# Left-over tokens of a head pair in both partition halves, and the last output tile stored by column halves

## The chip, the cores and the metric

The kernel runs on one core of one Trainium2 chip. A core has a matmul engine (TensorE, PE in the profile, with its weight loads listed apart as PEld), a vector engine (VectorE, DVE), a scalar engine (ScalarE, ACT), GpSimd (POOL) and SyncE (SP), which here only issues transfers. Operands lie in on-chip memory of 128 partitions (SBUF); matmuls write to a second on-chip memory of 128 partitions (PSUM), which is divided into banks of 512 fp32 values a partition. The metric is the device time of one execution in microseconds (us), the median of several.

## What is computed

Attention with a softmax on q along the head dimension and one on k along the tokens, and behind it a two-layer network on all tokens:

```python
batch, n_heads, seq, head_dim = (8, 8, 576, 64)
q_s = softmax(q, axis=-1); k_s = softmax(k, axis=2)          # each with + 1e-09 in the denominator
kv = np.einsum('bhsd,bhse->bhde', k_s, v)
attn = np.einsum('bhsd,bhde->bhse', q_s, kv)
x = attn.transpose(0, 2, 1, 3).reshape(4608, 512)
r = np.maximum(x @ w_in, 0.0)                                # w_in 512 x 2048
out = (s * (r * r) + b) @ w_out                              # w_out 2048 x 512
```

All of it is fp32. A head has 576 tokens: four tiles of 128 and a left-over of 64 (`LEFT`).

## The kernel before

**The network.** The 4608 tokens are worked on as eight blocks of 512 tokens (`TB`), one for each batch, and a ninth block that collects the 64 left-over tokens of all eight batches. A block takes 16 steps, one for each 128 columns of w_in. A step is twelve 128x512 matmuls for `h` (L998: four chunks of the contraction, three products each, since every fp32 operand is split in a high and a low part) and twelve for the output, `acc` (L1061). Between them ACT takes the relu of h (L1023), DVE squares and scales (L1036), ACT rounds to the high part gh (L1038) and DVE takes the rest gl (L1040). In the last full block and the ninth, h is made by products of half-size blocks (L875), and the ninth block's output by `final` (L984).

**Attention** is done beside that, one block ahead. Heads come in "pairs" of transfers, `pr` = 0 to 15, of four heads each (two units `u`, two heads in each). `load_heads` and `load_v` (L284 to L298) bring k, q and v of a pair from memory into one tile each: token tiles 0 to 3 in all 128 partitions, and the left-over tile `NQ` (= 4) of all four heads in partitions 0 to 63. Partitions 64 to 127 of that tile are held at zero by memsets (L294, L499, L578), so that a matmul over all 128 partitions adds nothing there. For pairs 2 to 15, `k_pair` and `k_late` take the maximum of k over the tokens in DVE steps (L472, then L475 and L476, or L508 and L509 where the second works on the left-over tile alone), subtract it (L491, L538) and take the exponential (L498, L576).

**The kv product** of a pair is `heads` (L306): for each of the two units i, for each of the five token tiles n, for each of the two heads h, one matmul with the tile's 128 partitions as contraction, 64 columns of k as weights and 65 columns of v (64 values and a column of ones, which gives the softmax's denominator) as the moving operand. That makes 20 fp32 matmuls, each of which the chip runs as two instructions, 40 in the trace. Head 0 writes to PSUM partitions 0 to 63 and head 1 to 64 to 127, so each uses one half of the array's columns. Both units' results lie in one bank, in the PSUM tile "sm". DVE (L654, L655, L661) scales the result into the block-diagonal kvf, ACT and POOL split it (L668, L670), and `x_late` multiplies it with the transposed q (xp and xq, L690) into a two-bank tile "big" and a one-bank tile "sm". Pairs 0 and 1 take another way (`k_stream`, `kv_stream`), in which k arrives transposed.

**The order** on each engine is not that of the code. Each piece of work is a generator that yields an `Op` with its engine, an estimated cost in us, a due step, the things it needs and the PSUM or SBUF tiles that it takes and frees. `Order.run` (L161) builds the program by always choosing the operation that can start earliest by these estimates, and among near ones the one with the earliest due step. So a changed cost or another tile moves other work as well. Each engine then runs its instructions strictly in that order, with semaphores for what it depends on.

**The end.** `leave_last(j)` (L1080) copies the finished PSUM tile j of the ninth block into SBUF, by ACT (by DVE for j = 2), and stores it as two transfers of 64 tokens each, 128 KB, one issued by SP and one by ACT.

Of the kernel before, what the change touches and what calls it, by code (L numbers as in the profile page):

```python
# [8 lines left out]
F32 = mybir.dt.float32  # L9
# [16 lines left out]
def attention_moe(ctx: ExitStack, tc: tile.TileContext, q, k, v, w_in, w_out, s, b, out):  # L26
# [257 lines left out]
    def load_heads(pr, which, eng, i=0, n=4):  # L284
# [2 lines left out]
        eng.dma_start(t[:, :, 0:NQ, :], main(src, i, n))  # L287
        eng.dma_start(t[0:LEFT, :, NQ, :], left(src, i, n))

    def load_v(pr):  # L290
        main, left = sources(pr)
        vt, rest = v_tile(tiles[pr][2])
        if pr == NP // 2:
            nc.gpsimd.memset(rest[LEFT:P, :, 0:D], 0.0)  # L294
            nc.gpsimd.memset(tiles[pr][2][:, 0:VW].rearrange("p (m e) -> p m e", e=D + 1)[:, :, D:D + 1], 1.0)
        for h in range(4):
            nc.sync.dma_start(vt[:, h, :, 0:D], main(v, h, 1)[:, 0])
        nc.sync.dma_start(rest[0:LEFT, :, 0:D], left(v, 0, 4))  # L298

    def copier(eng):  # L300
        return nc.scalar.copy if eng == "ACT" else nc.vector.tensor_copy
# [4 lines left out]
    def heads(kv, kt, vt):  # L306

        for i in range(2):
            for n in range(NT):
                for h in range(2):  # L310
                    nc.tensor.matmul(  # L311
                        kv[h * D:(h + 1) * D, i], kt[:, i, h, n], vt(2 * i + h, n), start=(n == 0), stop=(n == NT - 1)
                    )

    def scales(z, src):

# [45 lines left out]
    def k_pair(pr):  # L362
        us = (2 * pr, 2 * pr + 1)
        due = DUE_K[us[0]]

        def sm(n):
            return ps.tile([P, 512], F32, name=f"{n}_{pr}", tag="sm", bufs=1)

        yield Op("DVE", 0.69, due, needs=[f"k{u} there" for u in us])
        kt = by_head(tiles[pr][0])  # L370
        kts = [kt[:, 2 * i:2 * i + 2] for i in range(2)]
        m2, m1, km = k_tiles(pr)
        k_max_2(kt, m2)
# [12 lines left out]
        for i, u in enumerate(us):  # L386
            yield Op("ACT", 0.63, due, gives=[f"k{u}"])
            k_exp(kts[i])

    def kv_second(pr):  # L390
        due = DUE_V[pr]
        yield Op("PE", 1.4, due, needs=[f"k{u}" for u in (2 * pr, 2 * pr + 1)] + [f"v{pr} there"], take=["sm"], gives=[f"kv{pr}"])
        kv = ps.tile([P, 512], F32, name=f"kv_{pr}", tag="sm", bufs=1)[:, 0:2 * (D + 1)].rearrange("p (u e) -> p u e", u=2)
        heads(kv, by_head(tiles[pr][0]).rearrange("p (u h) n d -> p u h n d", u=2), v_at(tiles[pr][2]))
# [3 lines left out]
        yield Op("ACT", 1.03, due, free=["sm"], gives=[f"kvf{pr}"])  # L398
        blocks(pr, kv[:, :, 0:D], z)

    def kv_stream(pr):
# [71 lines left out]

    def k_max_1(kt, m2, m1):
        nc.vector.tensor_tensor(out=m1, in0=m2[:, :, 0], in1=m2[:, :, 1], op=ALU.max)  # L475
        nc.vector.tensor_tensor(out=m1[0:LEFT], in0=m1[0:LEFT], in1=kt[0:LEFT, :, NQ], op=ALU.max)  # L476

    def k_turn(m1, kT):
        for i in range(2):
# [14 lines left out]
            op=ALU.subtract,  # L494
        )

    def k_exp(kt):
        nc.scalar.activation(kt, kt, AF.Exp)  # L498
        nc.gpsimd.memset(kt[LEFT:P, :, NQ], 0.0)  # L499


    maxima = {}
# [1 line left out]
    def k_max_0(kt, m2, m1):  # L504

        m2, kt = [t.rearrange("p h n (r t) -> p h n t r", t=2) for t in (m2, kt)]
        m1 = m1.rearrange("p h (t r) -> p h t r", t=2)
        nc.vector.tensor_tensor(out=m1, in0=m2[:, :, 0], in1=m2[:, :, 1], op=ALU.max)  # L508
        nc.vector.tensor_tensor(out=m1[0:LEFT], in0=m1[0:LEFT], in1=kt[0:LEFT, :, NQ], op=ALU.max)  # L509

    def k_turn_0(m2, m1):
        m = m2.rearrange("p h n d -> p (h n d)")[:, 0:4 * D]
# [58 lines left out]
    def k_exps(u):  # L571
        pr, i = divmod(u, 2)
        due = begin(pr)
        yield Op("ACT", 0.72, due, needs=[f"k{u} less"])
        kt = by_head(tiles[pr][0])[:, 2 * i:2 * i + 2]
        nc.scalar.activation(kt, kt, AF.Exp)  # L576
        yield Op("POOL", 0.2, due, gives=[f"k{u}"])
        nc.gpsimd.memset(kt[LEFT:P, :, NQ], 0.0)  # L578

    def q_late(u):  # L580
        pr, i = divmod(u, 2)
# [62 lines left out]
    def kv_late(pr):  # L644
        us = (2 * pr, 2 * pr + 1)
        due = begin(pr)
        yield Op("PE", 1.52, due - NFC, needs=[f"k{u}" for u in us] + [f"v{pr} there"], take=["sm"], gives=[f"kv{pr}"], late=WAIT)

        kt, _, vt = tiles[pr]
        kv = ps.tile([P, 512], F32, name=f"kv_{pr}", tag="sm", bufs=1)[:, 0:2 * (D + 1)].rearrange("p (u e) -> p u e", u=2)  # L650
# [5 lines left out]

        kvf = kvfs[pr % 2]
        for h in range(2):
            yield Op("DVE", 0.5, due, needs=[f"x{u - 4}" for u in us], free=["sm"] if h else ())
# [420 lines left out]
    def leave_last(j):  # L1080

        t = B * NFC + NFC * (j + 1)

        yield Op("DVE" if j == 2 else "ACT", 0.6, t, needs=[f"final {j}"])
        if not lasts:
            lasts.append(work.tile([P, AREA], F32, name="last", tag="area"))
        o = lasts[0][:, j * DO:(j + 1) * DO]
        (nc.vector.tensor_copy if j == 2 else nc.scalar.copy)(o, acc[B, j])  # L1088
        for i, (e, eng) in enumerate((("SP", nc.sync), ("ACT", nc.scalar))):
            yield Op(e, 0.1, t)  # L1090
            bb = 2 * j + i
            eng.dma_start(out[bb * S + TB:(bb + 1) * S, :], o[half[i]])
# [35 lines left out]
    def whole(pr, which, n, due=0, needs=()):  # L1128
        gives = [f"k{2 * pr} there", f"k{2 * pr + 1} there"] if which == 0 else [f"{n}{pr} there"]
        yield Op("SP", 1.3, due, needs=needs, gives=gives, kb=576)  # L1130
        load_heads(pr, which, nc.sync)

    def others():

# [21 lines left out]
    def reload(pr):  # L1156
# [2 lines left out]
        due = DUE_K[2 * pr] - 2  # L1159

        def v_():
            yield Op("SP", 3.2, due, needs=[f"kv{p}"], gives=[f"v{pr} there"], kb=1100)
# [4 lines left out]
    def reload_late(pr):  # L1167
# [3 lines left out]
        late = [f"q{u} turned" if pr > NP else f"qe{u}" for u in (2 * pr - 2, 2 * pr - 1)]  # L1171

        def k_():
            yield Op("SP", 1.3, due, needs=gone, gives=[f"ks{pr} there"], kb=576)
            load_heads(pr, 0, nc.sync)

        def q_():
            yield Op("SP", 1.3, due, needs=gone + late, gives=[f"q{pr} there"], kb=576)
            load_heads(pr, 1, nc.sync)

        def v_():
            yield Op("SP", 3.2, due, needs=gone, gives=[f"v{pr} there"], kb=864)
            load_v(pr)

        return k_(), q_(), v_()
# [67 lines left out]
```

## Time and profile before

| | |
|---|---|
| median of 3 runs | 859.88 us (859.0 to 860.23) |
| the profiled execution, device time | 860.12 us |
| the profiled execution, span from the first to the last instruction | 858.2 us |
| DVE, ACT, POOL busy | 590.8, 435.7, 164.4 us |
| HBM read and written | 60.29 and 18.40 MB, 92 GB/s over the span |

The device time of the profiled execution is 1.9 us more than its span. Busy times are the sums of the instructions of an engine; matmuls overlap in the pipeline, so their durations (about 390 ns for one of 128x512) are longer than the distance from one to the next, and what counts for the time is that distance, read from the starts. The rows that the argument rests on stand in the prediction.

### The profile page before, as it was taken

The numbers are of one execution on the slowest core, as the hardware profiler recorded it, in microseconds if no ns is written. First come the engines' busy times: TensorE is split into PE (matmuls) and PEld (weight loads), VectorE is DVE, ScalarE is ACT, GpSimd is POOL, SyncE is SP. The second block draws the span as 40 slices with busy tenths as digits, with TensorE's granted clock in tenths as the row PEclk, the third lists the DMA queues.
The fourth block names the chain that finished last, engine by engine and source line by source line (L and its number), as shares of the span: only waits on it lengthen the run. The fifth ranks groups of instructions, "written<-read, shape, count | busy, mean of one in ns | idle before, by whom it ended". The sixth has DMA issues, their size and how long they took to land.

```text
span 858.2 us, 11838 instructions
## 1 busy us (share of the span) xinstructions
PE 846.7 (99%) x4406; PEld 699.5 (82%) x4406; DVE 590.8 (69%) x922; ACT 435.7 (51%) x733; POOL 164.4 (19%) x184
## 2 busy tenths in 40 slices
PE   8899999999999999999999999999999999999997
PEld 6688888888888888888888888888888888888886
DVE  6999976778685857777587867685766587656300
ACT  5898744446364535454544454454336665555300
POOL 1000011111121110211020202120023436665000
PEclk9999999999999999999999999999999999999999
DMA  9994134334333324333424314421530110000100
GB/s 262 303 379 145 34 87 138 83 94 104 115 85 86 84 89 132 90 83 89 132 77 97 90 68 93 123 61 50 132 90 1 53 50 0 1 1 1 49 25 25
DMA packets 106573, 79.47 MB, mean 93 GB/s; under 512 B 56212, under 2 KB 100244, under 8 KB 106388
## 3 DMA queue, kind: packets, MB, share of 16 engines
q1 hardware_dynamic: 105364, 77.60, 32.4%
q10 hardware_dynamic: 1152, 1.11, 0.4%
q8 instruction: 35, 0.57, 0.3%
q14 instruction: 22, 0.18, 0.1%
HBM read 60.29 MB, written 18.40 MB: 92 GB/s over the span
## 4 chain that ended last, share of the span: by engine, by line
PE 94%; DMA 3%; DVE 1%; ACT 1%; issue 0%; SPq 0%; ACTq 0%
PE acc L1061 41%; PE h L998 35%; PE q L875 8%; PE last L984 5%; PE kv L311 2%; PE qa L875 1%; DMA st<-in_moe_w_out_dram 1%; DMA raw<-in_q_dram 1%; PE xp L690 1%; PE xq L690 1%; DMA area<-in_q_dram 1%; PE xp L454 0%; DVE low L232 0%; PE qT L444 0%; DVE w L239 0%
## 5 line engine op out<-in xcount | busy, mean ns | idle before, releaser
L998 PE MATMUL h<-x,w 128*128 128x512 f32 x1344 | 329.5, 391 | 0.8 <-DVE x L463 0.8
L1061 PE MATMUL acc<-w,gh 128*128 128x512 f32 x1024 | 317.7, 391 | 0.0
L998 PEld LDWEIGHTS h<-x,w 128*128 128x128 f32 x1344 | 250.1, 188 | 53.2 <-DVE x L463 1.4
L1061 PEld LDWEIGHTS acc<-w,gh 128*128 128x128 f32 x1024 | 190.9, 188 | 39.4
L1061 PE MATMUL acc<-w,gl 128*128 128x512 f32 x512 | 199.6, 390 | 0.1
L1023 ACT ACTIVATE r<-h 128x512 f32<-128x512 f32 x112 | 66.8, 596 | 170.8 <-PE h L998 168.3
L1036 DVE SCALAR_TENSOR_TENSOR r<-r,sb 128x512 f32<-128x512 f32 x106 | 84.5, 798 | 92.2 <-ACT r L1023 91.7
L1061 PEld LDWEIGHTS acc<-w,gl 128*128 128x128 f32 x512 | 96.1, 188 | 20.6 <-DVE gl L1040 0.5
L1038 ACT ACTIVATE gh<-r,sb 128x512 fp32r<-128x512 f32 x106 | 76.7, 724 | 53.8 <-DVE r L1036 52.9
L1040 DVE SCALAR_TENSOR_TENSOR gl<-r,sb,gh 128x512 fp32r<-128x512 f32 x106 | 83.2, 785 | 29.5 <-ACT gh L1038 28.6
L589 POOL TENSOR_TENSOR area<-area,qm 128x640 f32<-128x640 f32 x24 | 33.5, 1399 | 134.8 <-DVE qm L587 119.4
L606 POOL TENSOR_TENSOR qe<-qe,qr 128x640 f32<-128x640 f32 x24 | 32.3, 1348 | 75.9 <-DVE qr L602 41.1
L984 PE MATMUL last<-w 128*128 128x512 f32 x192 | 43.7, 389 | 0.0
L984 PEld LDWEIGHTS last<-w 128*128 128x128 f32 x192 | 36.1, 188 | 7.5
L670 POOL TENSOR_TENSOR spare<-kvf,spare 128x256 fp32r<-128x256 f32 x12 | 9.8, 820 | 129.9 <-issue 119.4
L696 ACT COPY y<-xp 64x320 f32<-64x320 f32 x48 | 20.2, 420 | 26.9 <-PE xp L690 26.5
L576 ACT ACTIVATE area<-area 128x640 f32<-128x640 f32 x24 | 17.6, 737 | 18.7 <-DVE area L538 18.7
L578 POOL MEMSET area<- 64x128 f32 x24 | 4.8, 200 | 116.2 <-issue 92.4
L958 DVE SCALAR_TENSOR_TENSOR gl<-r,sb,gh 128x512 fp32r<-128x512 f32 x16 | 13.7, 855 | 17.1 <-ACT gh L953 17.1
L700 DVE TENSOR_TENSOR y<-xp,y 64x320 f32<-64x320 f32 x48 | 23.4, 488 | 2.7 <-ACT y L696 1.7
L1088 DVE COPY last<-last 128x512 f32<-128x512 f32 x1 | 0.7, 692 | 34.6 <-PE last L984 34.6
L311 PEld LDWEIGHTS kv<-area 128*64 128x64 f32 x600 | 18.7, 137 | 5.1 <-issue 3.3
(190 smaller groups left out, 1073.4 us busy)
## 6 DMA issues: line engine op xcount, KB each, us to landing
st<-in_moe_w_in_dram SPq DMA_DIRECT2D x16, 512.0 KB, 8.3
st<-in_moe_w_out_dram SPq DMA_DIRECT2D x16, 512.0 KB, 9.0
out_dram<-o SPq DMA_DIRECT2D x16, 512.0 KB, 2.6
turned<-area SPq DMA_DIRECT2D x24, 320.0 KB, 2.3
qT<-turned SPq DMA_DIRECT2D x48, 160.0 KB, 3.1
area<-in_q_dram SPq DMA_DIRECT2D x14, 512.0 KB, 5.4
area<-in_k_dram SPq DMA_DIRECT2D x14, 512.0 KB, 4.3
area<-in_v_dram SPq DMA_DIRECT2D x56, 128.0 KB, 5.0
```

The source lines that it names most:

```text
L311: nc.tensor.matmul(kv[h * D:(h + 1) * D, i], kt[:, i, h, n], vt(2 * i + h, n), start=(n == 0), stop=(n == NT - 1))
L589: nc.gpsimd.tensor_tensor(out=qt, in0=qt, in1=bc(qm, [P, 2, NT, D]), op=ALU.subtract)
L606: nc.gpsimd.tensor_tensor(out=qe_, in0=qe_, in1=qr, op=ALU.mult)
L700: nc.vector.tensor_tensor(out=y[half[h], at], in0=parts[h][a][half[h]], in1=y[half[h], at], op=ALU.add)
L875: nc.tensor.matmul(BANK[where], w(a)[:, c * P:(c + 1) * P], xs[b_][:, c], start=k in (0, 1, 3) and n == 0, stop=n == 5, skip_group_check=True)
L984: nc.tensor.matmul(t_, g[:, js], w_, start=(f == 0 and i == 0), stop=(f == NFC - 1 and i == 2))
L998: nc.tensor.matmul(hp_, w[:, j, c, :], x[:, c, :], start=(c == 0 and i == 0), stop=(c == NP - 1 and i == 2))
L1023: nc.scalar.activation(r, hp_, AF.Relu)
L1036: nc.vector.scalar_tensor_tensor(out=r, in0=r, scalar=s_col, in1=r, op0=ALU.mult, op1=ALU.mult)
L1038: nc.scalar.activation(gh, r, AF.Identity, bias=b_col)
L1040: nc.vector.scalar_tensor_tensor(out=gl, in0=r, scalar=b_col, in1=gh.bitcast(F32), op0=ALU.add, op1=ALU.subtract)
L1061: nc.tensor.matmul(acc[blk, j // 2][:, j % 2], g[:, js], w_, start=(f == 0 and i == 0), stop=(f == NFC - 1 and i == 2))
```

## The change

Two things are changed.

First, for pairs 2 to 15, the left-over tile of k and v no longer lies in partitions 0 to 63 for all four heads. Heads 0 and 1 (unit i = 0) stay there, heads 2 and 3 (unit i = 1) go to partitions 64 to 127 (`half[i]`). Each of the two left-over transfers (k's and v's) becomes two, of two heads each. The kv product, now `heads_by_rows`, first does the 16 matmuls over 128 partitions (unit 0, then unit 1) and then the four left-over ones, each over the 64 partitions that hold its tokens. A 64-partition contraction with 64 weight columns uses a quarter of the array (64x64), and the four use four different quarters. The units' results now lie in two different banks: the product takes the two-bank tile "big" in place of "sm". The maximum over the left-over tile (L476, L509) becomes two DVE instructions of 64x128 in place of one of 64x256. The memset of v's unused half at pair 2 (L294) goes; k's memsets (L499, L578) stay and zero the other half. The estimated costs follow: the kv product 1.4 to 1.27 and 1.52 to 1.39, the loads with 0.65 more for each added transfer.

Second, the last output tile (j = 3) is copied by column halves, 256 columns by ACT and 256 by DVE, and each half leaves as one transfer of 128 tokens with 1 KB each, ACT's half issued by ACT and DVE's by SP.

```diff
+    def load_k(pr):
+        main, left = sources(pr)
+        t = by_head(tiles[pr][0])
+        nc.sync.dma_start(t[:, :, 0:NQ, :], main(k, 0, 4))
+        for i in range(2):
+            nc.sync.dma_start(t[half[i], 2 * i:2 * i + 2, NQ, :], left(k, 2 * i, 2))
+
     def load_v(pr):
...
-            nc.gpsimd.memset(rest[LEFT:P, :, 0:D], 0.0)
...
-        nc.sync.dma_start(rest[0:LEFT, :, 0:D], left(v, 0, 4))
+        for i in range(2):
+            nc.sync.dma_start(rest[half[i], 2 * i:2 * i + 2, 0:D], left(v, 2 * i, 2))
...
+    def heads_by_rows(kv, kt, vt):
+
+        at = [(i, n, h, slice(0, P)) for i in range(2) for n in range(NQ) for h in range(2)]
+        at += [(i, NQ, h, half[i]) for i in range(2) for h in range(2)]
+        for i, n, h, rows in at:
+            nc.tensor.matmul(
+                kv[h * D:(h + 1) * D, i], kt[rows, i, h, n], vt(2 * i + h, n)[rows], start=(n == 0), stop=(n == NQ)
+            )
...
     def kv_late(pr):
...
-        yield Op("PE", 1.52, due - NFC, needs=[f"k{u}" for u in us] + [f"v{pr} there"], take=["sm"], gives=[f"kv{pr}"], late=WAIT)
+        yield Op("PE", 1.39, due - NFC, needs=[f"k{u}" for u in us] + [f"v{pr} there"], take=["big"], gives=[f"kv{pr}"], late=WAIT)
...
-        kv = ps.tile([P, 512], F32, name=f"kv_{pr}", tag="sm", bufs=1)[:, 0:2 * (D + 1)].rearrange("p (u e) -> p u e", u=2)
-        heads(kv, by_head(kt).rearrange("p (u h) n d -> p u h n d", u=2), v_at(vt))
+        kv = ps.tile([P, 2, 512], F32, name=f"kv_{pr}", tag="big")[:, :, 0:D + 1]
+        heads_by_rows(kv, by_head(kt).rearrange("p (u h) n d -> p u h n d", u=2), v_at(vt))
...
-        nc.vector.tensor_tensor(out=m1[0:LEFT], in0=m1[0:LEFT], in1=kt[0:LEFT, :, NQ], op=ALU.max)
+        k_max_left(kt, m1)
+
+    def k_max_left(kt, m1):
+        for i in range(2):
+            m, rest = m1[half[i], 2 * i:2 * i + 2], kt[half[i], 2 * i:2 * i + 2, NQ]
+            nc.vector.tensor_tensor(out=m, in0=m, in1=rest, op=ALU.max)
...
-        nc.gpsimd.memset(kt[LEFT:P, :, NQ], 0.0)
+        nc.gpsimd.memset(kt[half[1 - i], :, NQ], 0.0)
...
     def leave_last(j):
...
+        if j == NQ - 1:
+            rows = out.rearrange("(b s) e -> b s e", b=B)[2 * j:2 * j + 2, TB:S]
+            for e, eng, copy, es in (
+                ("ACT", nc.scalar, nc.scalar.copy, slice(0, DO // 2)), ("SP", nc.sync, nc.vector.tensor_copy, slice(DO // 2, DO))
+            ):
+                copy(o[:, es], acc[B, j][:, es])
+                yield Op(e, 0.1, t)
+                eng.dma_start(rows[:, :, es], o[:, es])
+            return
```

The same edits are made in `kv_second` (pairs 2 and 3) and in `k_exp`, `k_exps` and `k_max_0`; `whole` and `reload_late` call `load_k` for k.

The instructions in their order show three places. The first is PE at the kv product of pair 2 (names end in tile numbers; "waits" lists the semaphores by the engine or transfer queue that raises them). Before:

```order
L311 MATMUL kv_913<-area 64x65 [waits DMAHW0_49,DVE_49,DMAHW2_49,PE_49,Activation_49]
L311 MATMUL kv_913<-area 64x65 [waits DMAHW3_49]
L311 MATMUL kv_913<-area 64x65 x6
L311 MATMUL kv_913<-area 64x65 [waits DMAHW6_49,DMAHW1_49,Pool_49]
L311 MATMUL kv_913<-area 64x65
L311 MATMUL kv_913<-area 64x65 [waits DMAHW4_49,Activation_49]
L311 MATMUL kv_913<-area 64x65 [waits DMAHW5_49]
L311 MATMUL kv_913<-area 64x65 x6
L311 MATMUL kv_913<-area 64x65 [waits Pool_49]
L311 MATMUL kv_913<-area 64x65
```

And in the changed kernel:

```order
L327 MATMUL kv_915<-area 64x65 [waits DMAHW3_49,DMAHW0_49,Activation_49]
L327 MATMUL kv_915<-area 64x65 [waits DMAHW4_49]
L327 MATMUL kv_915<-area 64x65 x6
L327 MATMUL kv_915<-area 64x65 [waits DMAHW5_49,Activation_49]
L327 MATMUL kv_915<-area 64x65 [waits DMAHW6_49]
L327 MATMUL kv_915<-area 64x65 x6
L327 MATMUL kv_915<-area 64x65 [waits DMAHW7_49,DMAHW1_49]
L327 MATMUL kv_915<-area 64x65
L327 MATMUL kv_915<-area 64x65 [waits DMAHW2_49,DMAHW0_49]
L327 MATMUL kv_915<-area 64x65
```

The number of matmuls is the same, 20; the left-over ones, which stood at the end of each unit, now stand together at the end, wait for their own transfers and no longer for POOL's memset.

The second is PE some 1.5 steps behind the kv product of pair 4, where the first product with that pair's q (xp, xq) stands. Before, behind the last of a step's four groups of acc:

```order
L1061 MATMUL acc_2_1457<-w_559,gh_1558 128x512 x2
L1061 MATMUL acc_2_1457<-w_559,gl_1559 128x512
L690 MATMUL xp_1620<-qhl,spare 128x320
L690 MATMUL xq_1621<-qhl,spare 128x256
L690 MATMUL xp_1620<-qhl,spare 128x320
L690 MATMUL xq_1621<-qhl,spare 128x256
L998 MATMUL h_1628<-x_977,w_661 128x512 x12
```

In the changed kernel, behind the first group of the same step:

```order
L1082 MATMUL acc_0_1450<-w_560,gh_1566 128x512 x2
L1082 MATMUL acc_0_1450<-w_560,gl_1567 128x512
L711 MATMUL xp_1618<-qhl,spare 128x320
L711 MATMUL xq_1619<-qhl,spare 128x256
L711 MATMUL xp_1618<-qhl,spare 128x320
L711 MATMUL xq_1619<-qhl,spare 128x256
L1082 MATMUL acc_0_1450<-w_560,gh_1566 128x512 x2
```

It stands nine 128x512 matmuls earlier, the kv product ahead of it three earlier, and the next xp and xq behind it twelve earlier. These three are all that the planner's new numbers put earlier on PE; the other moves there put an attention product later, by three to fifteen matmuls.

The third is the end of the program on ACT and DVE: `last` on the left of the arrow is the SBUF tile, on its right the PSUM tiles of the four parts. Before, ACT (DVE's last instruction there is the copy of the third part):

```order
L1088 COPY last<-last_7058 128x512 [waits PE_49]
L1092 DMA out_dram<-last 64x512 [waits Activation_49]
L1092 DMA out_dram<-last 64x512 [waits DVE_49]
L1088 COPY last<-last_7163 128x512 [waits PE_49]
L1092 DMA out_dram<-last 64x512 [waits DMAHW1_49,Activation_49]
```

In the changed kernel, ACT:

```order
L1118 COPY last<-last_7099 128x512 [waits PE_49]
L1122 DMA out_dram<-last 64x512 [waits Activation_49]
L1122 DMA out_dram<-last 64x512 [waits DVE_49]
L1114 COPY last<-last_7204 128x256 [waits PE_49]
L1116 DMA out_dram<-last 2x64x256 [waits DMAHW5_49,Activation_49]
```

And DVE:

```order
L979 SCALAR_TENSOR_TENSOR gl_7016<-r_6997,sb,gh_7015 128x512 [waits PE_49,Activation_49]
L962 SCALAR_TENSOR_TENSOR misc<-misc,sb 128x512 [waits Activation_49]
L979 SCALAR_TENSOR_TENSOR w_1124<-misc,sb,w_1124 128x512 [waits Activation_49]
L1118 COPY last<-last_7152 128x512 [waits PE_49]
L1114 COPY last<-last_7204 128x256 [waits Activation_49]
```

DVE's new copy of the second half waits for ACT, whose copy of the first half stands ahead of it in the program, and not for PE.

More of the change, by code (lines that the diff above doesn't have):

```diff
@@ L387, in k_pair @@
             yield Op("ACT", 0.63, due, gives=[f"k{u}"])
-            k_exp(kts[i])
+            k_exp(kts[i], i)
     def kv_second(pr):
         due = DUE_V[pr]
-        yield Op("PE", 1.4, due, needs=[f"k{u}" for u in (2 * pr, 2 * pr + 1)] + [f"v{pr} there"], take=["sm"], gives=[f"kv{pr}"])
-        kv = ps.tile([P, 512], F32, name=f"kv_{pr}", tag="sm", bufs=1)[:, 0:2 * (D + 1)].rearrange("p (u e) -> p u e", u=2)
-        heads(kv, by_head(tiles[pr][0]).rearrange("p (u h) n d -> p u h n d", u=2), v_at(tiles[pr][2]))
+        yield Op("PE", 1.27, due, needs=[f"k{u}" for u in (2 * pr, 2 * pr + 1)] + [f"v{pr} there"], take=["big"], gives=[f"kv{pr}"])
+        kv = ps.tile([P, 2, 512], F32, name=f"kv_{pr}", tag="big")[:, :, 0:D + 1]
+        heads_by_rows(kv, by_head(tiles[pr][0]).rearrange("p (u h) n d -> p u h n d", u=2), v_at(tiles[pr][2]))
         yield Op("DVE", 0.33, due)
@@ L397, in kv_second @@
         scales(z, kv[:, :, D])
-        yield Op("ACT", 1.03, due, free=["sm"], gives=[f"kvf{pr}"])
+        yield Op("ACT", 1.03, due, free=["big"], gives=[f"kvf{pr}"])
         blocks(pr, kv[:, :, 0:D], z)
@@ L495, in k_less, with k_exp @@
         )
-    def k_exp(kt):
+    def k_exp(kt, i):
         nc.scalar.activation(kt, kt, AF.Exp)
-        nc.gpsimd.memset(kt[LEFT:P, :, NQ], 0.0)
+        nc.gpsimd.memset(kt[half[1 - i], :, NQ], 0.0)
     maxima = {}
@@ L508, in k_max_0 @@
         nc.vector.tensor_tensor(out=m1, in0=m2[:, :, 0], in1=m2[:, :, 1], op=ALU.max)
-        nc.vector.tensor_tensor(out=m1[0:LEFT], in0=m1[0:LEFT], in1=kt[0:LEFT, :, NQ], op=ALU.max)
+        k_max_left(kt, m1)
     def k_turn_0(m2, m1):
@@ L577, in k_exps @@
         yield Op("POOL", 0.2, due, gives=[f"k{u}"])
-        nc.gpsimd.memset(kt[LEFT:P, :, NQ], 0.0)
+        nc.gpsimd.memset(kt[half[1 - i], :, NQ], 0.0)
     def q_late(u):
@@ L646, in kv_late @@
         due = begin(pr)
-        yield Op("PE", 1.52, due - NFC, needs=[f"k{u}" for u in us] + [f"v{pr} there"], take=["sm"], gives=[f"kv{pr}"], late=WAIT)
+        yield Op("PE", 1.39, due - NFC, needs=[f"k{u}" for u in us] + [f"v{pr} there"], take=["big"], gives=[f"kv{pr}"], late=WAIT)
         kt, _, vt = tiles[pr]
-        kv = ps.tile([P, 512], F32, name=f"kv_{pr}", tag="sm", bufs=1)[:, 0:2 * (D + 1)].rearrange("p (u e) -> p u e", u=2)
-        heads(kv, by_head(kt).rearrange("p (u h) n d -> p u h n d", u=2), v_at(vt))
+        kv = ps.tile([P, 2, 512], F32, name=f"kv_{pr}", tag="big")[:, :, 0:D + 1]
+        heads_by_rows(kv, by_head(kt).rearrange("p (u h) n d -> p u h n d", u=2), v_at(vt))
         yield Op("DVE", 0.5, due)
@@ L658, in kv_late @@
         for h in range(2):
-            yield Op("DVE", 0.5, due, needs=[f"x{u - 4}" for u in us], free=["sm"] if h else ())
+            yield Op("DVE", 0.5, due, needs=[f"x{u - 4}" for u in us], free=["big"] if h else ())
             for g in range(2):
@@ L1130, in whole @@
         yield Op("SP", 1.3, due, needs=needs, gives=gives, kb=576)
-        load_heads(pr, which, nc.sync)
+        if which == 0:
+            load_k(pr)
+        else:
+            load_heads(pr, which, nc.sync)
     def others():
@@ L1161, in v_ @@
         def v_():
-            yield Op("SP", 3.2, due, needs=[f"kv{p}"], gives=[f"v{pr} there"], kb=1100)
+            yield Op("SP", 3.85, due, needs=[f"kv{p}"], gives=[f"v{pr} there"], kb=1100)
             load_v(pr)
@@ L1173, in k_ @@
         def k_():
-            yield Op("SP", 1.3, due, needs=gone, gives=[f"ks{pr} there"], kb=576)
-            load_heads(pr, 0, nc.sync)
+            yield Op("SP", 1.95, due, needs=gone, gives=[f"ks{pr} there"], kb=576)
+            load_k(pr)
         def q_():
@@ L1181, in v_ @@
         def v_():
-            yield Op("SP", 3.2, due, needs=gone, gives=[f"v{pr} there"], kb=864)
+            yield Op("SP", 3.85, due, needs=gone, gives=[f"v{pr} there"], kb=864)
             load_v(pr)
```

## The prediction

> **What bounds the kernel now.** I read the page first, then who waited for whom on PE, then PE's timeline around one kv product, then the end.
>
> ```profile
> span 858.2 us, 11838 instructions
> PE 846.7 (99%) x4406; PEld 699.5 (82%) x4406; DVE 590.8 (69%) x922; ACT 435.7 (51%) x733; POOL 164.4 (19%) x184
> ...
> PEclk9999999999999999999999999999999999999999
> ...
> PE 94%; DMA 3%; DVE 1%; ACT 1%; issue 0%; SPq 0%; ACTq 0%
> ```
>
> PE is busy for 99% of the span at the full granted clock, and the chain that ended last is PE for 94%. A busy PE may still wait inside, so the next view is PE's waits:
>
> ```profile
> PE unused L1201 <- POOL ident masks.py:199: 2.5, 1, 2.5
> PE kn L355 <- ACT early L350: 1.8, 2, 1.6
> PE xp L454 <- ACT early L447: 1.1, 2, 0.7
> PE h L998 <- DVE x L463: 0.8, 2, 0.6
> PE kn L355 <- DVE x L463: 0.5, 1, 0.5
> ```
>
> These five rows are all. Asked for the first 46 us alone the view gives the same rows, and from 46 us to the end none. So from 46 us on PE waits for nobody: the time is the sum of the distances from one matmul to the next, plus what follows the last one. The change is worth what it does to those two, unless it makes PE wait.
>
> **The kv product as it is.** PE's timeline and weight loads around the product of one late pair (pair 8; columns: start, length, engine, line, operation, shape, count), and the groups of its line:
>
> ```profile
> 325.53 0.39 PE L998 MATMUL h<-x,w 128*128 128x512 f32 x1
> ...
> 325.84 1.39 PE L311 MATMUL kv<-area 128*64 128x65 f32 x40
> 327.16 0.73 PE L1061 MATMUL acc<-w,gh 128*128 128x512 f32 x2
> 327.73 0.39 PE L1061 MATMUL acc<-w,gl 128*128 128x512 f32 x1
> 327.96 0.62 PE L1061 MATMUL acc<-w,gh 128*128 128x512 f32 x2
> 328.42 0.40 PE L1061 MATMUL acc<-w,gl 128*128 128x512 f32 x1
> 328.65 0.62 PE L1061 MATMUL acc<-w,gh 128*128 128x512 f32 x2
> ...
> 325.84 0.19 PEld L311 LDWEIGHTS kv<-area 128*64 128x64 f32 x3 [0.35 <-issue]
> ...
> 326.89 0.20 PEld L311 LDWEIGHTS kv<-area 128*64 128x64 f32 x4
> ...
> L311 PEld LDWEIGHTS kv<-area x600: 132/138/139, 17.6 to 643.5; 128*64 128x64 f32 x150
> L311 PE MATMUL kv<-area x600: 218/222/272, 17.6 to 643.5; 128*64 128x65 f32 x140, 128*64 128x64 f32 x10
> ```
>
> - A 128x512 matmul takes 0.23 us from start to start: 327.96 to 328.65 is 0.69 for three.
> - The 40 kv instructions run two by two. The last four loads span 0.20 us at 0.138 each; at equal distances they would be 0.02 apart, and 40 would start within 0.8 us. But 1.39 less the 0.22 of one instruction is 1.17 from the first start to the last, which is 19 distances of 0.06 and a little; so they start in pairs, 0.06 apart. One **beat** (two instructions side by side in the two column halves) is 0.06 us.
> - The change of the array's shape costs on both sides. Into it: from h at 325.53 to kv at 325.84 is 0.31 in place of 0.23, since kv's first weights were not loaded ahead (the 0.35 before the load row), and the first kv matmul takes 272 ns where the median is 222. That is 0.08 + 0.05 = 0.13. Out of it: the last kv start, 325.84 + 1.17 = 327.01, to acc at 327.16 is 0.15 in place of a beat's 0.06; and the first three acc take 0.80 (327.16 to 327.96) in place of 0.69. That is 0.09 + 0.11 = 0.20.
>
> **What the first edit does to it.** Of 20 beats, 16 stay. The four left-over matmuls, eight instructions, took 4 beats two by two. Over 64 partitions each uses its own quarter of the array; if all four run side by side, as the column halves do now, they take 2 beats. Gain: 2 x 0.06 = 0.12 us a pair. More than that the beats can't give, for the two passes of one matmul in one quarter follow each other.
>
> Against it stands a third change of shape inside the product, from 128x64 to 64x64. No row of this trace shows that one. From below it costs nothing (the column halves are the same, only the rows are divided, and the loads could run ahead). From above it costs what the way out costs, 0.20. The nearest row is the same start of a wait behind a kv matmul: 0.15 in place of 0.06 until the array is empty, 0.09, and then a load of 64 columns that nothing hides, 0.05 as on the way in. I take 0.14, because both shape changes that the trace shows, in either direction, wait for the array and for the first load. The way out of 64x64 I take as the way out now. Each pair then gets 0.14 - 0.12 = **0.02 slower**, 14 pairs (560 of the 600 rows above have 65 columns, 40 a pair) 0.3 us. The bounds are -0.12 x 14 = -1.7 us and, with four beats kept and 0.20 for the change of shape, +2.8 us.
>
> The Trainium skill bears on this in "TensorEngine Tiling (Array Packing)", section "Tiling Modes", "Key Properties": changing the tiling mode, and not only the tile, drains the engine. For the two changes of shape in this trace that agrees (0.15 in place of 0.06); no run here shows one between 128x64 and 64x64, which that page lists as different modes. By the rule the product ends up where I have it, and without it 1.7 us lower.
>
> **What lies beside.** These edits cost nothing as long as PE is fed, and the rows show by how much it is:
>
> ```profile
> 187.36 0.20 POOL L578 MEMSET area<- 64x128 f32 x1 [0.48 <-PE h L998]
> ...
> 190.00 0.28 PE L311 MATMUL kv<-area 128*64 128x65 f32 x2
> ...
> 153.14 0.60 SPq L288 DMA_DIRECT2D area<-in_k_dram  x1
> ...
> 158.36 0.74 SPq L298 DMA_DIRECT2D area<-in_v_dram  x1
> ...
> 162.01 0.68 DVE L472 TENSOR_TENSOR misc<-area 128x512 f32<-128x512 f32 x1
> ...
> L509 DVE TENSOR_TENSOR misc<-misc,area 64x256 f32<-64x256 f32 x12 | 5.0, 418 | 0.4
> ...
> L360 DVE COPY area<-kn 64x128 f32<-64x128 f32 x1 | 0.3, 273 | 0.0
> ...
> 159.26 0.74 POOL L670 TENSOR_TENSOR spare<-kvf,spare 128x256 fp32r<-128x256 f32 x1 [10.51 <-ACT spare L668]
> ...
> 161.59 0.31 PE L690 MATMUL xp<-qhl,spare 128*128 128x320 f32 x1
> ```
>
> - The maximum: two instructions of 64x128 in place of one of 64x256 at 0.42. The nearest half-size row is 0.27, so +0.12 a pair on DVE (at most +0.42, if half the size saves nothing). It delays k's chain, which for pair 5 ended at 187.56 with kv at 190.00: 2.4 us of cover. Without cover it would be 14 x 0.12 = 1.7 us.
> - One more issue each for k and v on SP: 0.60 and 0.74. What stands behind it in SP's queue are q's and v's loads and the store of the maxima. k's loads were issued by 153.74 and first used at 162.01, so there is room for several such issues.
> - POOL's memset no longer holds the product up; it did not before, as nothing on PE waited.
> - The product takes "big" in place of "sm". xp takes both, so either way one excludes the other.
> - Order: pair 4's first xp stands 9 x 0.23 = 2.1 us earlier, and its input was ready at 160.00, 1.6 us ahead. That leaves 0.5 us short, were it not that kv stands 3 x 0.23 = 0.7 earlier and its chain with it. I take 0, and keep 0.5 for the range.
>
> **The end.** The rows of the last part, and of the copies that give a half-size one:
>
> ```profile
> 853.68 0.58 ACT L1088 COPY last<-last 128x512 f32<-128x512 f32 x1 [21.17 <-PE last L984]
> 854.29 0.47 SPq L1092 DMA_DIRECT2D out_dram<-last  x1
> 854.30 0.50 ACTq L1092 DMA_DIRECT2D out_dram<-last  x1
> ...
> out_dram<-last SPq DMA_DIRECT2D x4, 128.0 KB, 2.4
> out_dram<-last ACTq DMA_DIRECT2D x4, 128.0 KB, 2.7
> ...
> L696 ACT COPY y<-xq 64x256 f32<-64x256 f32 x48 | 17.6, 367 | 0.9
> ...
> L1073 DVE COPY o<-acc 128x1024 f32<-128x1024 f32 x6 | 7.3, 1225 | 5.4 <-PE acc L1061 5.4
> ...
> L1088 DVE COPY last<-last 128x512 f32<-128x512 f32 x1 | 0.7, 692 | 34.6 <-PE last L984 34.6
> ```
>
> ACT's half takes 0.37 in place of 0.58, so its transfer is issued at 854.09 and lands 2.7 later, at 856.8 (now 857.0). DVE's half waits for ACT's copy. 512 columns more cost DVE 1.225 - 0.692 = 0.53, so 256 fewer leave 0.692 - 0.27 = 0.42. It starts some 0.03 behind ACT's end (as SP does now, 854.26 to 854.29) and ends at 854.50; SP's transfer leaves at 854.53 and lands 2.4 later, at 856.9. The end moves from 857.0 to 856.9: **-0.1 us**. If the two copies ran at once it would be -0.2; if the packets of 1 KB cost more than those of 2 KB, 0 to +0.2.
>
> **Sum.** +0.3 - 0.1 = +0.2 us. The profiled execution took 860.12 us, 1.9 above its span, and would take 860.3; it lies 0.24 above the median of 859.88. I predict 860.1 us, no change that can be told: a measurement of this kernel tells about 0.2%, 1.7 us, from none.
>
> **Rivals.**
> - *The change of shape is free.* Then each pair gains the whole 0.12: -1.7 - 0.1 = -1.8, 858.1 us. For it: the column halves stay, and the loads of a beat run ahead within the product. Against: at both changes that the trace shows, the loads stopped running ahead. Partly free, with only the load unhidden (0.05), it would be -1.1: 858.8. The Trainium skill, "TensorE: Matmul & The Clock Gate", Part 3, "The mechanism", speaks for this rival: a weight load for another row group is pulled ahead of matmuls in flight, and tiles overlap. The loads of the column halves here, in pairs, agree; no row shows another row group.
> - *The four do not run side by side.* Two by two they take the 4 beats of now, and the change of shape comes on top: 14 x 0.14 = +2.0, less 0.1: 861.8 us, slower. It decides from the point where the shape change costs more than what is saved in beats. For it: the trace shows two side by side, never four; if the passes are interleaved in twos, the third and fourth begin one beat late, 3 beats, +0.08 x 14 = +1.1: 860.9. Against: the four use separate quarters and two banks.
> - *PE waits somewhere.* k's chain or xp comes late: up to 0.5 us at the places above, 860.6.
>
> **Chances.** Forecast 0.5; shape change free 0.18, partly free 0.09; four not side by side 0.07, three beats 0.11; a new wait 0.05. Between the cases lie 858.1 and 861.8. The range of 858.2 to 861.5 leaves out half of the free case and most of the two-by-two case, some 0.15 with the runs' own scatter of 0.6. Faster by over 0.2% (below 858.2) holds about half of the free case and some unknown gain at the end: 0.14. Slower by over 0.2% (above 861.6) holds the two-by-two case and a larger wait: 0.11. Within: 0.75.
>
> **What would show it.** In the changed trace, the 32 instructions of the full-height part should have the beat of now; then a gap of 0.15 instead of 0.06 before the first left-over matmul, with its load not ahead; then eight instructions in two beats, starts in fours. From the last h before kv to the first acc behind it a product should take about what it takes now, 1.63 us (325.53 to 327.16). At 1.5 the change of shape is free; at 1.75 the four went two by two. PE's waits behind 46 us should stay empty, and the last DVE copy should start at the end of ACT's. I am wrong if rows on PE's waits appear for kv or xp, or if the gap before the left-over part is a beat.

## The result, and the profile after

| | before | after |
|---|---|---|
| median of 5 runs | 859.67 us | 865.33 us (864.73 to 866.19) |
| the profiled execution, device time and span | 860.12, 858.2 us | 865.45, 863.7 us |
| ratio of the times | | 1.0066, 95% interval 1.0052 to 1.008 |

The changed kernel is 5.7 us slower, and the forecast was 860.1 with a range up to 861.5. The page of the changed kernel (span; busy time, share and instructions of each engine; shares of the chain that ended last):

```profile
span 863.7 us, 11887 instructions
...
PE 846.9 (98%) x4406; PEld 698.2 (81%) x4406; DVE 594.3 (69%) x937; ACT 436.1 (50%) x733; POOL 165.7 (19%) x183
...
PE 94%; DMA 3%; DVE 1%; ACT 0%; issue 0%; SPq 0%; ACTq 0%
```

PE is as busy as before (846.7), over a span 5.4 us longer (863.65 and 858.24). So either PE now waits, or it has stopped earlier than the span ends. PE's waits in the changed kernel (line waited for: us in total, times, longest):

```profile
PE unused L1234 <- POOL ident masks.py:199: 2.5, 1, 2.5
PE kn L371 <- ACT early L366: 2.3, 2, 2.0
PE xp L470 <- ACT early L463: 1.1, 2, 0.7
PE h L1019 <- DVE x L479: 0.6, 2, 0.5
PE kn L371 <- DVE x L479: 0.5, 1, 0.5
```

These are the five rows of before, and again none lies behind 46 us. That leaves the distances between matmuls and the end. The timeline of the changed kernel's end (start, length):

```profile
852.65 1.52 PE L1005 MATMUL last<-w 128*128 128x512 f32 x6
852.88 0.87 PEld L1005 LDWEIGHTS last<-w 128*128 128x128 f32 x4
854.21 0.37 ACT L1114 COPY last<-last 128x256 f32<-128x256 f32 x1 [21.17 <-PE last L1005]
854.62 1.09 ACTq L1116 DMA_DIRECT2D out_dram<-last  x1
854.62 0.42 DVE L1114 COPY last<-last 128x256 f32<-128x256 f32 x1 [10.59 <-ACT last L1114]
855.07 0.60 SPq L1116 DMA_DIRECT2D out_dram<-last  x1
```

Everything is issued by 855.7, yet the span ends at 863.7. SP, which waits for the last transfers, says for what. Its waits from 850 us on, first of before, then of the changed kernel:

```profile
SPq L1248 <- DMA out_dram<-last: 2.1, 2, 1.8
SPq L1248 <- PEq L1248: 0.9, 2, 0.7
```

```profile
SPq L1281 <- DMA out_dram<-last: 6.9, 2, 5.0
SPq L1281 <- PEq L1281: 0.6, 2, 0.4
```

The transfers end late. In the trace's semaphore events ACT's lands at 860.81 and SP's at 862.76, which is 6.2 and 7.7 us behind their issue, where before the last two landed 2.6 and 2.3 us behind theirs. How they are carried shows in the view of the transfers from 855 to 864 us, before and after (all packets, then those of each queue):

```profile
DMA packets 161, 0.27 MB, mean 30 GB/s; under 512 B 32, under 2 KB 32, under 8 KB 160
...
q1 hardware_dynamic: 80, 0.13, 7.3%
q10 hardware_dynamic: 80, 0.13, 3.8%
```

```profile
DMA packets 260, 0.26 MB, mean 29 GB/s; under 512 B 4, under 2 KB 260, under 8 KB 260
...
q10 hardware_dynamic: 130, 0.13, 5.2%
q1 hardware_dynamic: 130, 0.13, 4.5%
```

Before, a transfer is 80 packets: 64 rows of 2 KB and 16 small ones (4 bytes in the trace, at the end of the transfer). After, it is 130: 128 rows of 1 KB and **2** small ones. The small packets are the writes to the semaphore. If each DMA engine that carries a part of a transfer makes one, 16 engines carried a transfer before and 2 carry it now. The packets' own times agree: of SP's transfer 13 to 17 packets were in flight at a time before (855.6 to 856.1), and mostly two are now (2.2 in the mean from 860.5 to 862.4). The bytes are the same.

For the accounts, I compared each matmul's start in the two traces, by its number. From 70 us to the last matmul PE falls back by 0.64 us; from the start of the last matmul to the end of the span it is 9.86 us (853.79 to 863.65) in place of 4.98 (853.26 to 858.24): +4.88. The first 70 us are 0.11 shorter. The sum is 5.4, the difference of the spans.

The 4.88 has two parts. The last landing comes 8.97 us behind the start of the last matmul in place of 3.68, +5.29; from that landing to the end of the span it is 0.90 us in place of 1.31, -0.41. The second part is not the store's: in the traces of all the experiments below this last stretch takes 1.27 to 1.34 us without the first edit and 0.84 to 0.97 with it. It goes with SP's wait for PE's queue (0.7 and 0.4 at the longest, above); why the first edit shortens it is not shown.

### The profile page after: what moved, and what is told of

The parts are those of the page before. It is cut to its first block, busy times and chain, and to the rows that moved or that the text cites. A ratio compares the mean times of both kernels' runs of the same rounds, so it can differ in the third digit from the quotient of the medians.

```text
span 863.7 us, 11887 instructions
## 1 busy us (share of the span) xinstructions
PE 846.9 (98%) x4406; PEld 698.2 (81%) x4406; DVE 594.3 (69%) x937; ACT 436.1 (50%) x733; POOL 165.7 (19%) x183
## 4 chain that ended last, share of the span: by engine, by line
PE 94%; DMA 3%; DVE 1%; ACT 0%; issue 0%; SPq 0%; ACTq 0%
PE acc L1082 41%; PE h L1019 35%; PE q L896 8%; PE last L1005 5%; PE kv L327 2%; PE qa L896 1%; DMA st<-in_moe_w_out_dram 1%; DMA raw<-in_q_dram 1%; PE xp L711 1%; PE xq L711 1%; DMA area<-in_q_dram 1%; PE xp L470 0%; DVE low L232 0%; PE qT L460 0%; DVE w L239 0%
## 5 line engine op out<-in xcount | busy, mean ns | idle before, releaser
L1061 DVE SCALAR_TENSOR_TENSOR gl<-r,sb,gh 128x512 fp32r<-128x512 f32 x106 | 79.9, 753 | 27.4 <-ACT gh L1059 26.4
L631 DVE STREAM_TRANSPOSE area<-qe 128x640 f32<-128x640 f32 x24 | 20.1, 838 | 8.0 <-POOL qe L627 8.0
L979 DVE SCALAR_TENSOR_TENSOR gl<-r,sb,gh 128x512 fp32r<-128x512 f32 x16 | 13.7, 854 | 17.1 <-ACT gh L974 17.1
```

What stands on the lines that cost most here:

```text
L1061: nc.vector.scalar_tensor_tensor(out=gl, in0=r, scalar=b_col, in1=gh.bitcast(F32), op0=ALU.add, op1=ALU.subtract)
```

## The experiments

**Theory.** The end costs some 5 us, since the column halves' pattern in memory has an outer dimension of 2 (two batches, 64 rows each) and so goes by 2 engines; the kv product costs 0.6 us. **Rivals** for the end: packets of 1 KB; the copies of ACT and DVE one behind the other; two transfers at once; something that the first edit moves.

**One half of the change alone.** `undo_tail` is the changed kernel with the last tile stored as before; `tail_only` is the kernel before with only the new store.

```diff
 undo_tail: after, without
-        if j == NQ - 1:
-            rows = out.rearrange("(b s) e -> b s e", b=B)[2 * j:2 * j + 2, TB:S]
...
-            return
 tail_only: before, with the same lines
```

> The changed kernel, its last output tile stored as before (one copy by ACT, two transfers of 64 tokens with 2 KB each). Theory (the loss is the end: each column-half transfer is carried by 2 DMA engines in place of 16): only the kv product's +0.04 us a pair is left, +0.6 us: 860.3 where before is 859.7, ratio 1.0007. Rival (the first edit costs the time in a way that the last matmul's start does not show, or the trace of the changed kernel is not typical): over 862.

> The kernel before with only the last tile stored by column halves. Theory (engines): the whole +4.9 us of the end, 864.6 where before is 859.7, ratio 1.0057; the last transfer lands over 7 us behind its issue, with 2 semaphore writes a transfer. Rival (the end is late because of what the first edit moves): within 1 us of before.

Measured: undo_tail 860.03 us, ratio to before 1.0005 (0.9996 to 1.0013); tail_only 864.87, ratio 1.0060 (1.0047 to 1.0072). The store alone makes the whole loss, and the first edit alone can't be told from nothing by its time.

**Outer dimension or packet size.** `tail_four` keeps the column halves and their 1 KB packets, but stores each half in two transfers of 64 rows. `tail_one` does the opposite: 2 KB packets, one copy, one transfer, but the outer dimension 2.

```diff
 tail_four
-                eng.dma_start(rows[:, :, es], o[:, es])
+                for g in range(2):
+                    eng.dma_start(rows[g, :, es], o[half[g], es])
 tail_one, in place of the loop over the halves
+            nc.scalar.copy(o, acc[B, j])
+            yield Op("SP", 0.1, t)
+            nc.sync.dma_start(out.rearrange("(b s) e -> b s e", b=B)[2 * j:2 * j + 2, TB:S], o)
```

> The changed kernel; each column half leaves as two transfers of 64 tokens (still 1 KB a packet, still ACT's copy ahead of DVE's), four in all. Theory (engines: the outer dimension of a transfer is 64 again, so 16 engines carry it): each lands 2.2 to 3 us behind its issue; with the copies one behind the other (+0.5) and a second issue on each queue (+0.5) the end is 0.5 to 1.0 later than before, and with the kv product's +0.6 it takes 860.8 to 861.4. Rival (packets of 1 KB are what costs): as late as the changed kernel or later, 865 to 866. Rival (the copies one behind the other): it would have to stay at 865 as well.

> The changed kernel; the last tile is copied by ACT alone (512 columns) and leaves as one transfer of 2 x 64 tokens with 2 KB each, issued by SP. Theory (engines: the outer dimension is 2): 2 semaphore writes, 64 packets of 2 KB on each of two engines; the two transfers of the changed kernel moved the same bytes over 6.6 us (855.86 to 862.42), so this one needs about as long and lands 7.5 to 8.5 us behind its issue: the end about as late as in the changed kernel, 864 to 866. Rival (1 KB packets, or two transfers at once, or the copies one behind the other): none of these is there any more, so the end is as before, 860.0 to 860.5.

Measured: tail_four 859.96 us, ratio 1.0004 (0.9995 to 1.0013); tail_one 864.99, ratio 1.0059 (1.0046 to 1.0071). The transfers of tail_four from 855 to 864 us (below them, KB and us from issue to landing; the first of ACT's two was issued ahead of 855), then those of tail_one with SP's wait:

```profile
DMA packets 320, 0.26 MB, mean 29 GB/s; under 512 B 64, under 2 KB 320, under 8 KB 320
...
out_dram<-last SPq DMA_DIRECT2D x2, 64.0 KB, 1.9
out_dram<-last ACTq DMA_DIRECT2D x1, 64.0 KB, 2.1
```

```profile
DMA packets 130, 0.26 MB, mean 29 GB/s; under 512 B 2, under 2 KB 2, under 8 KB 130
```

```profile
SPq L1277 <- DMA out_dram<-last: 7.1, 1, 7.1
```

In tail_four 256 packets of 1 KB go with 4 x 16 semaphore writes and land as fast as before. So 1 KB packets are no cause, nor are the copies one behind the other, since tail_four keeps both. tail_four even came out below what I had expected (860.8 to 861.4): its last landing comes 3.85 us behind the start of the last matmul, where in undo_tail, with the same product and the old store, it comes 3.67 behind. So the second issue on each queue adds little; the transfers land sooner (1.9 to 2.1). In tail_one there is one transfer with 2 KB packets and 2 semaphore writes, and it is as slow as the changed kernel. Nor is it that one transfer covers all 128 partitions; the stores of the earlier blocks do so too, and in the kernel before they land within 2.6 us:

```profile
out_dram<-o SPq DMA_DIRECT2D x16, 512.0 KB, 2.6
```

The outer dimension is the cause.

**Do the two transfers share their engines?** In `tail_mixed` ACT's half leaves in one transfer as in the changed kernel, DVE's in two of 64 rows.

```diff
+                if e == "ACT":
+                    eng.dma_start(rows[:, :, es], o[:, es])
+                    continue
+                for g in range(2):
+                    eng.dma_start(rows[g, :, es], o[half[g], es])
```

> The changed kernel; ACT's column half leaves as one transfer of 2 x 64 tokens as in the changed kernel, DVE's half as two transfers of 64 tokens. Theory (both transfers of the changed kernel went over the same two engines, about 20 KB a us for each): alone on them, ACT's 64 KB an engine take 3.3 us and land some 4.6 behind the issue, not 6.2; the end is 2.0 to 2.6 later than before, 862.1 to 862.8. Rival (each transfer has two engines of its own, and the length is that of one transfer by itself): ACT's lands 6.2 behind its issue as in the changed kernel, the end 3.7 to 4.0 later, 863.8 to 864.2.

Measured: 862.73 us, ratio 1.0034 (1.0021 to 1.0048), as the theory had it, though ACT's transfer took longer than expected: it landed 5.6 us behind its issue (854.28 to 859.89), where I had 4.6 and the rival 6.2. Its landing alone would not decide, but that of SP's transfers does (KB, us from issue to landing, in the view from 855 to 864 us):

```profile
out_dram<-last SPq DMA_DIRECT2D x2, 64.0 KB, 4.5
```

With the same shape they took 1.9 in tail_four. The semaphore events show why: of the 16 writes of the second one, 14 land by 858.54 and the last 2 at 859.98 and 860.07, behind the 859.89 of ACT's transfer. Those two engines were busy with ACT's half. So ACT's two engines are among the 16 that carry SP's transfers, and ACT's was slowed by SP's parts. Two transfers with the outer dimension 2, one on each queue, meet on the same two engines: in the changed kernel, from 858.66 to 860.42, packets of ACT's and of SP's half, some 35 of each, start in turn, and both queues together have 2.1 packets in flight in the mean, no more than ACT's alone ahead of that (2.1) or SP's alone behind it (2.2).

**The number, with other divisors.** `rows_dose` cuts the first of the two 64-row transfers of the tiles j = 0, 1, 2, whose stores lie beside later matmuls.

```diff
+            at = bb * S + TB
+            if i == 0 and j < 3:
+                m = (62, 63, 61)[j]
+                eng.dma_start(out[at:at + m, :], o[0:m])
+                eng.dma_start(out[at + m:at + LEFT, :], o[m:LEFT])
+                continue
```

> The kernel before; of the two 64-token transfers of the output tiles j = 0, 1, 2 the first is cut: 62 + 2 tokens for j = 0, 63 + 1 for j = 1, 61 + 3 for j = 2 (2 KB each; the end is untouched). Theory (the number of engines is the largest number up to 16 that divides the outer dimension): 2, 9 and 1 semaphore writes; at 20 KB a us for an engine 62 tokens take 3.1 us and land 4.5 to 5 behind the issue, 63 land 2 to 2.6 behind it, 61 take 6.1 us and land 7.5 to 8.5 behind it. Rival (only the two-batch pattern of the column halves is slow, not the outer number): all three land 2 to 2.7 behind their issue.

The issues on SP's queue (start, length), then the packets of the three windows in which they land, with the uncut half among them (64 rows and 16 writes):

```profile
821.13 0.27 SPq L1095 DMA_DIRECT2D out_dram<-last  x1
...
832.01 0.28 SPq L1095 DMA_DIRECT2D out_dram<-last  x1
...
843.00 0.23 SPq L1095 DMA_DIRECT2D out_dram<-last  x1
```

```profile
DMA packets 148, 0.26 MB, mean 48 GB/s; under 512 B 20, under 2 KB 20, under 8 KB 148
```

```profile
DMA packets 154, 0.26 MB, mean 57 GB/s; under 512 B 26, under 2 KB 26, under 8 KB 154
```

```profile
DMA packets 149, 0.28 MB, mean 33 GB/s; under 512 B 20, under 2 KB 20, under 8 KB 148
```

Less the 16 writes of the uncut half there are 4, 10 and 4: 2 + 2 for 62 and 2 rows, 9 + 1 for 63 and 1, 1 + 3 for 61 and 3. These are the largest divisors up to 16. By the semaphore events 62 rows landed at 825.74, 63 at 834.00 and 61 at 850.61, that is 4.6, 2.0 and 7.6 us behind the issue. Three rows fewer than 64 make the same store three times as long.

**The kv product.** All four kernels here store the last tile as before. `kv_full` keeps the new places of the tokens but multiplies over all 128 partitions; `left_first` puts the four left-over matmuls ahead; `left_twice` issues them twice; `left_split` puts two behind each unit. In left_twice the left-over tokens count twice in the result.

```diff
 kv_full
-        at = [(i, n, h, slice(0, P)) for i in range(2) for n in range(NQ) for h in range(2)]
-        at += [(i, NQ, h, half[i]) for i in range(2) for h in range(2)]
+        at = [(i, n, h, slice(0, P)) for i in range(2) for n in range(NT) for h in range(2)]
 left_first
+        at = [(i, NQ, h, half[i]) for i in range(2) for h in range(2)]
+        at += [(i, n, h, slice(0, P)) for i in range(2) for n in range(NQ) for h in range(2)]
 left_twice
+        at += 2 * [(i, NQ, h, half[i]) for i in range(2) for h in range(2)]
 left_split
+        for i in range(2):
+            at += [(i, n, h, slice(0, P)) for n in range(NQ) for h in range(2)]
+            at += [(i, NQ, h, half[i]) for h in range(2)]
```

(kv_full also sets the other half of v's left-over tile to zero at pair 2; start and stop follow the order.)

> The changed kernel with the last tile stored as before, and the kv product as before: all 20 matmuls over 128 partitions (the other half of a left-over tile holds zeros), but with the left-over tokens where the change puts them, so that the split maximum, the added transfers and the two-bank tile stay. Theory (beside PE these edits cost nothing): the block from the last h before kv to the first acc behind is 1.63 us again, no new row on PE's waits, and the time is that of before, 859.4 to 860.0. Rival (some of the change's cost lies in the added issues or the split maximum): the block is 1.63 and the time still above before, or PE waits.

> The changed kernel with the last tile stored as before; the four left-over matmuls stand ahead of the sixteen full ones. Theory (every change of shape waits for the array to be empty, in either direction): the same number of changes, so the block from h to the first acc stays at 1.68 us (1.66 to 1.70), with 0.15 between the last left-over matmul and the first full one. Rival (only the change to the smaller rows costs, the way back to 128 rows runs on): the block is 1.68 - 0.14 = 1.54 and the time 2 us below before.

> The changed kernel with the last tile stored as before; the four left-over matmuls are issued twice, so the left-over tokens count twice in the result. Their first two beats are 0.108 apart in the changed kernel, and so are the first two of the full part, where the following ones are 0.058 apart. Theory (the first beat behind a change of shape is long because its loads are not ahead; later ones are as short as the others, four side by side): two more beats of 0.058, block 1.68 + 0.12 = 1.79 us, time +1.6 on the changed kernel without its tail, 862. Rival (a beat of four 64x64 tiles always takes 0.108): block 1.89, time +3.0.

> The changed kernel with the last tile stored as before; each unit's two left-over matmuls stand behind that unit's eight full ones, so that they run two side by side and a product has two more changes of shape. Theory (each change costs 0.15 of gap in place of 0.06, and 0.05 more on its first beat; additive): h to the first acc is 0.318 + 0.465 + 0.149 + 0.115 + 0.149 + 0.465 + 0.149 + 0.115 + 0.149 = 2.07 us in place of 1.68, +0.40 a pair, +5.5 us, 865.5. Rival (most of a change's cost is hidden when the next tile uses other rows): 1.68 + 0.13 for the lost side-by-side, 1.8, 862.

PE's timeline around one product of the changed kernel:

```profile
417.74 0.84 PE L1019 MATMUL h<-x,w 128*128 128x512 f32 x3
418.51 1.43 PE L327 MATMUL kv<-area 128*64 128x65 f32 x40
419.87 0.73 PE L1082 MATMUL acc<-w,gh 128*128 128x512 f32 x2
```

and of kv_full, left_first, left_twice and left_split, in this order:

```profile
457.46 1.39 PE L327 MATMUL kv<-area 128*64 128x65 f32 x40
458.78 1.20 PE L1019 MATMUL h<-x,w 128*128 128x512 f32 x4
```

```profile
457.75 1.43 PE L327 MATMUL kv<-area 64*64 64x65 f32 x40
459.11 0.72 PE L1019 MATMUL h<-x,w 128*128 128x512 f32 x2
```

```profile
458.35 1.54 PE L327 MATMUL kv<-area 128*64 128x65 f32 x48
459.82 0.96 PE L1019 MATMUL h<-x,w 128*128 128x512 f32 x3
```

```profile
81.09 1.83 PE L329 MATMUL kv<-area 128*64 128x65 f32 x40
82.85 0.99 PE L1021 MATMUL h<-x,w 128*128 128x512 f32 x3
```

From the first kv start to the next other matmul it is 1.36 us in the changed kernel, 1.32 in kv_full (and before: 325.84 to 327.16), 1.36 in left_first, 1.47 in left_twice and 1.76 in left_split. With the 0.318 from the last h to kv these are 1.68, 1.64, 1.68, 1.79 and 2.08. The starts of single instructions, the same in each of a kernel's products (pairs 2 to 15) within 2 ns:

```
ns                   h to kv   within full   to left-over   within left-over   out to h/acc   sum
before                 318        1164            -               -                152        1634
after                  318         933           149             127               149        1676
left_first             318         934        148 (back)         128               150        1678
left_twice             318         933           149             245               148        1793
left_split             318     467 + 466      3 x 149         114 + 114            149        2075
```

- **left_first**: 148 ns before the left-over part's successor, as before its first matmul. The change of shape costs in both directions; the rival would have had a beat's 51 there. Time 860.53 us, ratio 1.0008 (0.9999 to 1.0017).
- **left_twice**: 118 ns for two more beats, 59 each, so four 64x64 tiles side by side take the beat of two 128x64 tiles. Only the first beat behind a change is long (0.108). Time 861.41, 1.4 above undo_tail, where 14 x 0.118 is 1.65.
- **left_split**: the pieces add up as expected, to 2.075. The time is 866.30, 6.3 above undo_tail where 14 x 0.40 is 5.6; in the traces each product came out 0.45 longer, 0.05 of it behind the product, in the first matmuls of the next shape.
- **kv_full**: 859.73 us, ratio 0.9998 (0.9990 to 1.0007). What lies beside PE (the split maximum, the added issues, the two-bank tile, pair 4's order) costs nothing that can be told.

The time of a whole run doesn't tell 0.6 us, since the first 70 us alone differ by up to 1.3 us from one trace to another. From 70 us to the last matmul traces differ less. How much later than in before PE gets over that stretch:

```
after +0.64   undo_tail +0.59   tail_four +0.62   tail_one +0.64   tail_mixed +0.64
tail_only 0.00   best_tail +0.02   rows_dose +0.02   kv_full +0.06
left_first +0.81   left_split +6.96
```

The first row has the new product, the second has not: +0.6 us, 14 x 0.042. (Of left_first's 0.2 us beyond that, 14 x 0.013 arise in the first dozen matmuls behind each product, not in the product itself.)

**A version that beats both?** From the last matmul to the end tail_four needs 4.7 us where before needs 5.0. `best_tail` is the kernel before with that store.

> The kernel before, its last tile copied by column halves and stored in four transfers of 64 tokens (the tail that was 0.25 us shorter from the last matmul to the end of the span, 4.69 in place of 4.94). Theory: 0.2 to 0.3 us faster than before, 859.5, ratio 0.9997, which the measurement can't tell from 1. Rival: the tail of that run was scatter, ratio 1.000.

Measured: 859.93 us, ratio 1.0001 (0.9992 to 1.0010): no difference. The 4.7 had been held against the wrong kernel. undo_tail, with the old store, needs 4.6: what is shorter is the stretch behind the last landing, and it came with the first edit. Up to the last landing the four transfers take 0.2 us more than the old store (3.87 us behind the start of the last matmul in best_tail, 3.68 in before). None of the versions run can be told to be faster than before.

## Why the prediction was wrong

**The step that failed is "The end".** I had it at -0.1 us, and its bound for what was not seen at "0 to +0.2" for packets of 1 KB. The copies were right: ACT's 0.37, DVE's 0.42, DVE's start at the end of ACT's. What failed is the next sentence, "SP's transfer leaves at 854.53 and lands 2.4 later". I took the landing time from rows of 64-row transfers and carried it over to a transfer of another shape, and the only thing that I priced about the shape was the packet's size, which costs nothing (tail_four). The measured term is +5.3 us up to the last landing (tail_only: +5.2 in time), and +4.9 up to the end of the span, since the stretch behind the landing is 0.4 shorter. Nothing in the trace of before showed a transfer with such a pattern, and that should have made it an operation to bound from both sides by its bytes per engine, not one to copy from a neighbour.

The Trainium skill, "DMA: Bandwidth & Descriptors", section "Why a DMA increments its semaphore by 16 and not by 1", states the rule: a transfer uses the largest number of engines up to 16 that divides the outermost dimension, other than 1, of both its sides. I didn't draw on it. The runs agree with it at each shape that was tried: 64 rows gave 16 semaphore writes, 63 gave 9, 62 gave 2, 61 gave 1, and the two-batch pattern 2. The page also says that a transfer issued from SP or ACT takes the lowest-numbered engines; that the changed kernel's two transfers met on the same two engines agrees, though the engines' numbers don't show in the traces.

**The first edit went as forecast, its size a little off.** PE kept no new wait. Into the left-over part the gap is 149 ns, as written (0.15), its load is not ahead (first beat 0.108, later ones 0.059 in left_twice), and the eight instructions start in two groups of four. That also rules out the partly free change of shape (by the gap) and the three beats (by the groups). The rival with a free change of shape is ruled out by left_first and left_split, which agree with the Trainium skill, "TensorEngine Tiling (Array Packing)", section "Tiling Modes", that a change of mode drains the engine (149 ns in place of 51); "the four do not run side by side" is ruled out by left_twice. The product was to take 0.02 longer and takes 0.042. Of the 22 ns that are missing, 7 are in the gap (I compared 0.15 with a beat of 0.06, but the last start of a beat is 7 ns behind its first, so 51 is what it replaces), 13 are the four starts of the last beat (20 ns apart from first to last, where two are 7), and the rest is rounding. Over 14 products it is +0.6 in place of +0.3 us. So this term alone would have stayed below what a measurement can tell (1.7 us), as forecast.

**What lies beside** cost nothing that can be told, as forecast (kv_full). That the first edit would shorten the stretch behind the last landing by 0.3 to 0.4 us stood in no term; kv_full has it too (0.97 us), so it doesn't come from the new product.

**The sum** with the measured terms: +0.6, +5.3 and -0.4 are +5.5 us, 865.4 on 859.9; measured 865.33. The range was too narrow for one reason: the bound on the end left out how a transfer is divided among engines.

## What to carry to other kernels

A store or load whose outermost dimension is small or has no large divisor up to 16 is carried by few DMA engines, and at the end of a kernel nothing hides it. Cut such a pattern into transfers with an outer dimension that 16 divides, even at the price of more issues (tail_four: 5.4 us back for two more). When a change gives a transfer a new shape, count its semaphore writes; and saving beats in the matmul array by a smaller shape only pays if it saves more than the change into that shape, here 0.15 us (98 ns of gap and 50 ns in the first beat behind it).

## What the runs showed of the hardware

- An engine alone moves little: 61 packets of 2 KB on one engine took 6.65 us from the first to the semaphore write, 19 KB a us; the two engines of tail_one moved 128 KB each in 6.3 us, 21 KB a us.
- The engines of such a transfer are shared with every other one: in rows_dose, while two engines carried 62 rows, the uncut half issued by ACT landed 14 of its 16 parts by 824.43 and the last two at 826.13.
- The length of an issue says nothing of this: the cut transfers were issued in 0.23 to 0.28 us, the column half on ACT's queue in 1.09.
